# Which chunks are streamed: a third value chunk for an output pair, and another chunk in PSUM

## The chip, the cores and the metric

The kernel runs on one core of one Trainium2 chip. The metric is the device time of the whole program in microseconds (us); lower is better. The median of three runs of the kernel before is 2106.07 us (2104.05 to 2109.13).

## What is computed

Two independent halves are concatenated. Half A is a long convolution done by FFT in matmul form; it fills the first part of the time and the change does not touch it. Half B is a recurrent attention over 64 segments of 32 tokens; each segment is attended together with 8 memory rows that the segment before has produced:

```python
for s in range(n_seg):                       # 64 segments, one after the other
    h = concat([mem, x[:, 32*s:32*s+32]])    # 8 memory rows + 32 tokens, width 1024
    q, k, v = h @ Wq, h @ Wk, h @ Wv         # 32 heads of 128 each
    p = softmax(mask(q @ k.T * 128**-0.5))
    o = (p @ v) @ Wo                         # back to width 1024
    mem = o[:, :8]
    outs.append(o[:, 8:])
```

The four weight matrices have 1024 x 4096 bf16 elements each, 8 MB apiece, 32 MB in all; each segment needs all of them, and not all fit on the chip.

## The kernel before

**Weights.** The weights are cut into pairs: tiles of 128 x 2 x 1024 bf16, 512 KB. There are 64: `("qk", g, i)`, the i-th of eight chunks of the query and key weights of head group g (four groups of eight heads); `("v", G, i)`, the i-th of eight chunks of the value weights of half G (heads of groups 2G and 2G+1); and `("o", g, i)`, the i-th of four output pairs of group g. Below, qk26 is `("qk", 2, 6)`, v05 is `("v", 0, 5)`, o32 is `("o", 3, 2)`. They are kept in three ways:

- 45 pairs are resident in SBUF for the whole loop.
- 17 pairs are streamed from DRAM in every segment (`STREAM`, L40): 7 of qk, 5 of v, 5 of o. The qk and o ones are read from copies `Wstqk`, `Wsto` that stage 2 writes in one piece each (`relay`, L122); the value ones straight from the input `Wv`.
- 2 pairs are parked in PSUM (`PARKED`, L41): v02 and qk16. In every segment ScalarE (L762) and VectorE (L763) each copy one half of such a pair from PSUM into the ring (`unpark`).

**Ring.** Streamed and parked pairs pass through a ring `wring` of five slots. When the PE has used a pair of the ring, `done` (L768) gives its slot away at once: `PARKED` names the pairs at whose use the slot goes to a parked pair (the copy is noted and done at the next `unpark()`); otherwise `place` (L686) issues the transfer of the next streamed pair on SP's queue. Streamed pairs come in the order of their use.

**Order of a segment** (written out by hand, L948 to L1034). The PE runs: qk of group 0; the first half of v (chunks 0 to 3); transposes of q and k of group 0 (`tr_a`); qk of group 1 chunks 0 to 3; scores of group 0; qk of group 1 chunks 4 to 7; v chunks 4 to 7; `tr_a` of group 1; qk of group 2, with the scores of group 1 in the middle and the first product of probabilities and values (`pv`, L901) behind; qk of group 3 with the scores of group 2; the second half of v with `pv(u1)` and the scores of group 3; then the output products (`wo`, L916) of groups 0 to 3 with `pv(u2)` and `pv(u3)` between them. Behind each score matrix a chain of VectorE and ScalarE follows: maximum and subtraction (L866, L867), exponentials (ScalarE, L875), sum, reciprocal, product, transpose (L879 to L884), and four block copies into `PB` (L894). ScalarE also evacuates the accumulators (`qks` L801, `vsb` L816, `OT` L905) and the segment's result `Y_sb` (L1026), whose transpose `mt_tp` (L935) gives the next segment's `hT` its memory rows. The next segment's tokens (tile `H`) come by a transfer that is issued after the last scores, and are transposed into `x_tp` (L927).

`unpark()` stands at two places of the segment: inside qk of group 0, behind its fifth chunk (for v02), and behind `tr_a` of group 0 (for qk16).

**First segment.** The last few resident output pairs (`n_o`) are loaded within segment 0, ahead of other transfers on SP's queue, at `first_loads(1)`, `(2)` and `(3)` (L950): three pairs.

Of the kernel before, what the change touches and what calls it, by code (L numbers as in the profile page):

```python
# [21 lines left out]
def fused_kernel(ctx: ExitStack, tc, q, k, v, shift_k, ssm_k, ssm_D, outa, x, mem0, Wq, Wk, Wv, Wo, outb, n_seg):  # L22
# [14 lines left out]
    NS = 17  # L37
    scale = 128.0 ** -0.5
    RING = 5
    STREAM = {"qk": ((2, 4), (3,), (2, 6), (2, 6)), "v": ((0, 3, 5), (1, 5)), "o": ((2,), (1,), (0, 3), (2,))}  # L40
    PARKED = {("qk", 0, 4): ("v", 0, 2), ("v", 0, 3): ("qk", 1, 6)}  # L41

    msched = tc.manual_schedule()
    msched.__enter__()
# [10 lines left out]
    def keys(m, g, r):  # L55
        return [(m, g, i) for i in r]
# [3 lines left out]
    pairs += [key for g in range(4) for key in keys("o", g, range(4))]  # L60
    streamed = [key for key in pairs if key[2] in STREAM[key[0]][key[1]]]
    parked = list(PARKED.values())
    resident = [key for key in pairs if key not in streamed and key not in parked]
# [38 lines left out]
    to_open = sorted(resident, key=lambda key: (key not in early, first.get(key, 96)))  # L102
    wide = {}

    def open_res(n):
        if n:
            pool = cw_.enter_context(tc.tile_pool(name=f"b_wres{len(to_open)}", bufs=1))
            if not wide:
                wide["t"] = pool.tile([128, 8, 2, 1024], BF, name="Wearly")
            for _ in range(n):  # L110
                res_pool[to_open.pop(0)] = pool
# [89 lines left out]
    def rows_view(ap2d, t):  # L201
        return ap2d.rearrange("(p r) d -> r p d", r=16)[t]
# [437 lines left out]
    with ExitStack() as c3:  # L640
        io = c3.enter_context(tc.tile_pool(name="a3_io", bufs=3, side="right"))
        wk = c3.enter_context(tc.tile_pool(name="a3_wk", bufs=2, side="right"))
        ps_big = c3.enter_context(tc.tile_pool(name="a3_ps", bufs=3, space=PSUM))
        open_res(6)
        zts = {}

        def load_z(t):
            if t < 16:
                zt = io.tile([128, 2, 1024], BF, tag="zt", name="zt")
                nc.sync.dma_start(zt[:], SZ.rearrange("m (h r) d -> r m h d", h=2)[t])  # L650
                qt = wk.tile([128, 1024], BF, tag="qt", name="qt", bufs=3)
                nc.sync.dma_start(qt[:], rows_view(q, t))
                zts[t] = zt, qt

        halves = [(key, n) for key in parked for n in range(2)]
        park_w = []
        load_z(0)
        load_z(1)
        rows.load_to(rows.at // 16 * 8 + 16)
        rows.go(4)  # L660
        for t in range(16):
            load_z(t + 2)
            rows.half(4 if t < 6 else 1)
            zt, qt = zts[t]
            pt = ps_big.tile([128, 1024], F32, tag="big", name="y_ps")
            for hf in range(2):
                for h in range(2):
                    nc.tensor.matmul(pt[:, hf * 512:(hf + 1) * 512], lhsT=G2h[h][:, :],
                                     rhs=zt[:, h, hf * 512:(hf + 1) * 512], start=(h == 0), stop=(h == 1))
            ot = wk.tile([128, 1024], BF, tag="ot", name="ot")  # L670
            nc.vector.tensor_tensor(out=ot[:], in0=pt[:], in1=qt[:], op=ALU.mult)
            if t == 14:
                rows.load_to(96)
                for key, n in halves:
                    park_w.append(pring.tile([128, 1024], BF, tag="pring", name="park_w"))
                    nc.sync.dma_start(park_w[-1][:], half_src(key, n))
            nc.sync.dma_start(rows_view(outa, t), ot[:])
# [48 lines left out]
            nc.sync.dma_start(t[n], half_src(key, n))  # L726

    late_o = [key for key in resident if key[0] == "o"]
    assert len(late_o) == 11 and len(to_open) == 11
    rows.half(6, "AD")  # L730
    for i, (key, n) in enumerate(halves):
        tw = ps_p.tile([128, 1024], BF, tag="pp", name="park_t")
# [15 lines left out]
    for key in late_o[:8]:  # L748
        to_open.remove(key)
    n_o = late_o[8:]  # L750
    open_res(3)
    act = cw_.enter_context(tc.tile_pool(name="b_act", bufs=1))
    act2 = cw_.enter_context(tc.tile_pool(name="b_act2", bufs=2))

# [4 lines left out]
    def unpark():  # L759
        while to_copy:  # L760
            key, t = to_copy.pop(0)
            nc.scalar.copy(t[:, 0, :], park[key][0][:])  # L762
            nc.vector.tensor_copy(t[:, 1, :], park[key][1][:])  # L763
# [4 lines left out]
    def done(key):  # L768
        if key in res:
            return  # L770
        if key in PARKED:
            t = ring.tile([128, 2, 1024], BF, tag="wring", name="wring")
            placed[PARKED[key]] = [t[:]]
            to_copy.append((PARKED[key], t))
        else:
# [38 lines left out]
    def v_out():  # L814
        v = act.tile([128, 2, 256], BF, tag="vsb", name="vsb")
        nc.scalar.copy(v[:].rearrange("p n x -> p (n x)"), vacc[0][:])  # L816
        return v
# [7 lines left out]
    def tr_a(u):  # L825
        tp = transposes(u.qks)
        tv = tp[:].rearrange("e (j t c r) -> e t c j r", j=4, t=2, c=2)
        QK = acte.tile([128, 8, 72], BF, tag="qks", name="QK")
        u.QT, u.KT = QK[:, :, 0:32], QK[:, :, 32:72]
        nc.gpsimd.tensor_copy(u.KT[:, :, 32:40], u.qkb.rearrange("e (h t r) -> e t h r", h=8, t=2)[:, 1])  # L830
        nc.scalar.copy(u.QT.rearrange("e (c j) r -> e c j r", c=2), tv[:, 0])  # L831
        nc.scalar.copy(u.KT[:, :, 0:32].rearrange("e (c j) r -> e c j r", c=2), tv[:, 1])
# [6 lines left out]
    def new_u(g):  # L839
        u = G()  # L840
        u.g = g
        u.qkb = qkb[:, g, :]
        return u
# [96 lines left out]
    def new_hT():  # L940
        return acte.tile([128, 8, 32], BF, tag="hT", name="hT")
# [6 lines left out]
    for s in range(n_seg):  # L948
        last = s + 1 == n_seg
        def first_loads(g):  # L950
            for key in (n_o[g - 1:g] if s == 0 and g else ()):
                for n in range(2):
                    res_half(key, n)

        first_loads(0)
        us = [new_u(g) for g in range(4)]
        u0, u1, u2, u3 = us
        qk_part(u0, range(0, 5))
        unpark()
        qk_part(u0, range(5, 8))  # L960
        qk_out(u0)
        v_part(0, range(0, 4))
        tr_a(u0)
        unpark()
        first_loads(1)
        qk_part(u1, range(0, 4))
        S = scores(u0)
        softmax(u0, S)
        if s == 0:
            nc.vector.memset(PB[:], 0.0)  # L970
        blocks(u0, "DDDD")
        qk_part(u1, range(4, 8))
        qk_out(u1)
        v_part(0, range(4, 8))
        tr_a(u1)
        u0.v = u1.v = v_out()
        first_loads(2)
        qk_part(u2, range(0, 4))
        S = scores(u1)
        softmax(u1, S)  # L980
        if last:
            spare = [key for key in resident if key[0] != "o" and key[1] < 1 + (key[0] == "qk") and key not in early]
            for key, at in zip([key for key in streamed if key[0] == "o"], spare):
                nc.sync.dma_start(res[at][:], Wst[key])
                res[key] = res[at]
            for s0, s1 in ((0, 32), (32, s)):
                nc.sync.dma_start(OLs[:, s0:s1].rearrange("e s h r -> e (s h r)"),
                                  OLd[:, s0:s1].rearrange("e s x -> e (s x)"))
        qk_part(u2, range(4, 8))
        qk_out(u2)  # L990
        pv(u0, s)
        blocks(u1, "DDDD")
        first_loads(3)
        qk_part(u3, range(0, 2))
        tr_a(u2)
        qk_part(u3, range(2, 6))
        S = scores(u2)
        softmax(u2, S)
        qk_part(u3, range(6, 8))
        qk_out(u3)  # L1000
        v_part(1, range(0, 1))
        pv(u1, s)
        blocks(u2, "DDDD")
        v_part(1, range(1, 2))
        tr_a(u3)
        v_part(1, range(2, 5))
        S = scores(u3)
        if not last:
            H = load_h(s + 1)
            qkb = load_b(s + 1)  # L1010
        softmax(u3, S)
        v_part(1, range(5, 8))
        u2.v = u3.v = v_out()
        Y = ps_a.tile([128, 512], F32, tag="a", name="yacc")
        wo(u0, Y)
        pv(u2, s)
        blocks(u3, "DDAA")
        wo(u1, Y)
        wo(u2, Y)
        pv(u3, s)  # L1020
        if not last:
            hT = new_hT()
            h_rows(H, hT, 8)
        wo(u3, Y)
        Y_sb = act.tile([128, 256], BF, tag="P", name="Y_sb")
        nc.scalar.copy(Y_sb[:], Y[:, 0:256])  # L1026
        if not last:
            fill_mem(hT, Y_sb)
        for dq in range(4):
            nc.gpsimd.dma_start(outb[32 * s:32 * s + 24, dq * 256:(dq + 1) * 256], Y_sb[32 * dq + 8:32 * dq + 32, :])  # L1030
        if not last:
            load_vb(s + 1)
# [88 lines left out]
```

## Time and profile before

| | before |
|---|---|
| median of three runs | 2106.07 us (2104.05 to 2109.13) |
| the profiled execution | 2093.32 us, span 2091.5 us, granted clock 0.984 |
| PE, DVE, ACT, POOL busy | 81%, 53%, 43%, 20% of the span |
| read from HBM, written | 673.5 MB, 56.6 MB: 349 GB/s over the span |
| transfers into the ring | 448 of Wstqk, 320 of Wv, 315 of Wsto, 512 KB each |
| copies from PSUM into the ring | 128 on ScalarE (mean 1021 ns), 128 on VectorE (mean 692 ns) |
| end of Y_sb of the first and of the last segment | 416.7 and 2025.4 us after the span's start |

The profile is of one execution, which was somewhat faster than the median of the runs. The loop over the segments takes about 1609 us from the first Y_sb to the last, 25.5 us for one segment; the rest is half A with the first loads, and a last stage (L1044) of some 60 us.

### The profile page before, as it was taken

To read this page: it belongs to the slowest core of one execution; us is meant where nothing else is said; L and a number is where in the kernel's file an instruction comes from. 1 tells how busy PE (TensorE), PEld (TensorE's weight loads), DVE (VectorE), ACT (ScalarE), POOL (GpSimd) and SP (SyncE) were. 2 spreads that over 40 slices of the span, in tenths; PEclk is the share of its full clock that TensorE was granted. 3 is DMA by queue.
4 is the path that set the end of the run, shared out by engine and by line. 5 is a ranking of instruction groups with operands and counts; after the bars stand their busy time and mean duration, and the time that the engine had idled before them with its cause. 6 is when DMAs were issued, how large, how long until landed. Compare 5 with 4: busy or idle time off the path is not lost. (4 is left out here: it accounts for less than half of the span.)

```text
span 2091.5 us, 73911 instructions
## 1 busy us (share of the span) xinstructions
PE 1702.4 (81%) x30484; PEld 894.2 (43%) x30514; DVE 1115.3 (53%) x3313; ACT 908.7 (43%) x2276; POOL 413.1 (20%) x1018
## 2 busy tenths in 40 slices
PE   5888987888788888888887878888888878888879
PEld 2433233444444444444444444444444444444449
DVE  6986833355555555555555555555555555555541
ACT  5556731244444444444444444444444444444430
POOL 2004730121111111111111111111212121111110
PEclk9999999999999999999999999999999999999999
DMA  6899989999999999999999999999999999999980
GB/s 236 282 346 362 343 287 381 352 377 372 356 375 368 365 360 370 372 366 375 358 368 353 367 358 372 359 377 358 371 358 378 363 352 351 374 370 379 368 337 23
DMA packets 266384, 728.64 MB, mean 348 GB/s; under 512 B 65007, under 2 KB 77183, under 8 KB 265277
## 3 DMA queue, kind: packets, MB, share of 16 engines
q1 hardware_dynamic: 239486, 686.65, 88.8%
q0 software_dynamic: 15520, 22.06, 3.3%
q10 hardware_dynamic: 11040, 15.21, 2.1%
q8 instruction: 239, 3.92, 0.7%
q14 instruction: 99, 0.81, 0.1%
HBM read 673.52 MB, written 56.56 MB: 349 GB/s over the span
## 5 line engine op out<-in xcount | busy, mean ns | idle before, releaser
L795 PE MATMUL qkacc<-Wqk,hT 128*32 128x512 bf16 x4096 | 338.5, 383 | 0.0
L795 PEld LDWEIGHTS <-hT 128*32 128x32 bf16 x8192 | 184.9, 96 | 236.3 <-issue 84.2
L916 PEld LDWEIGHTS <-OT 128*32 128x32 bf16 x8192 | 210.1, 96 | 109.5 <-issue 59.2
L795 PE MATMUL qkacc<-wring,hT 128*32 128x512 bf16 x2048 | 204.9, 389 | 31.3 <-DMA wring<-Wstqk 25.5
L763 DVE COPY wring<-park 128x1024 bf16<-128x1024 bf16 x128 | 88.6, 692 | 239.4 <-PE vacc L809 124.8
L875 ACT ACTIVATE P<-S 128x128 bf16<-128x128 f32 x256 | 71.1, 278 | 330.4 <-DVE S L867 244.3
L809 PE MATMUL vacc<-Wv,hT 128*32 128x512 bf16 x2560 | 209.8, 382 | 0.0
L809 PE MATMUL vacc<-wring,hT 128*32 128x512 bf16 x1536 | 154.7, 387 | 65.5 <-DMA wring<-in_B_Wv_dram 63.6
L809 PEld LDWEIGHTS <-hT 128*32 128x32 bf16 x4096 | 113.0, 95 | 184.4 <-issue 108.3
L762 ACT COPY wring<-park 128x1024 bf16<-128x1024 bf16 x128 | 130.7, 1021 | 138.9 <-PE qkacc L795 112.8
L894 DVE COPY PB<-P 32x160 bf16<-32x160 bf16 x896 | 172.9, 193 | 10.6
L879 DVE TENSOR_REDUCE sm<-P 128x4 f32<-128x256 bf16 x256 | 107.5, 420 | 128.6 <-ACT P L876 128.6
L831 ACT COPY QK<-tp 128x256 bf16<-128x256 bf16 x256 | 95.4, 373 | 185.7 <-PE tp L822 184.5
L795 PE MATMUL qkacc<-Wearly,hT 128*32 128x512 bf16 x2048 | 161.0, 391 | 18.4 <-DVE hT L936 17.9
L830 POOL COPY QK<-qkb 128x64 bf16<-128x64 bf16 x256 | 61.3, 239 | 564.5 <-PE tp L822 404.8
L916 PE MATMUL yacc<-wring,OT 128*32 128x256 bf16 x2520 | 126.7, 274 | 37.4 <-DMA wring<-Wsto 35.2
L905 ACT CAST OT<-otacc 128x256 bf16<-128x256 f32 x256 | 98.7, 386 | 130.4 <-PE otacc L901 130.4
L801 ACT CAST qks<-qkacc 128x512 bf16<-128x512 f32 x256 | 151.1, 590 | 4.2 <-PE qkacc L795 3.5
L1030 POOL DMA_DIRECT2D out_dram<-Y_sb x256 | 129.1, 511 | 84.8 <-ACT Y_sb L1026 82.8
L822 PE MATMUL tp<-ident,qks 128*128 128x128 bf16 x1024 | 102.4, 223 | 52.6 <-ACT qks L801 50.3
L866 DVE TENSOR_REDUCE mx<-S 128x4 f32<-128x160 f32 x256 | 83.2, 325 | 85.2 <-PE S L863 79.5
L901 PE MATMUL otacc<-PB,vsb 128*128 128x160 bf16 x512 | 97.6, 238 | 35.3 <-ACT vsb L816 35.3
(212 smaller groups left out, 2957.1 us busy)
## 6 DMA issues: line engine op xcount, KB each, us to landing
wring<-Wstqk SPq DMA_DIRECT2D x448, 512.0 KB, 6.2
wring<-in_B_Wv_dram SPq DMA_DIRECT2D x320, 512.0 KB, 6.7
wring<-Wsto SPq DMA_DIRECT2D x315, 512.0 KB, 6.3
SK<-s_sb SPq DMA_DIRECT2D x8, 1024.0 KB, 5.5
SU<-s_sb SPq DMA_DIRECT2D x8, 1024.0 KB, 8.9
QKBd<-stq ACTq DMA_DIRECT2D x4, 2048.0 KB, 9.5
Kg<-SK SPq DMA_DIRECT2D x16, 512.0 KB, 7.0
Ug<-SU SPq DMA_DIRECT2D x16, 512.0 KB, 8.3
```

The source lines that it names most:

```text
L762: nc.scalar.copy(t[:, 0, :], park[key][0][:])
L795: nc.tensor.matmul(u.qk[p0:p0 + 32, :], lhsT=hT[:, kc, :], rhs=w[:, t, c2 * 512:(c2 + 1) * 512], start=(kc == 0), stop=(kc == 7), tile_pos ...
L801: nc.scalar.copy(u.qks[:], u.qk[:])
L809: nc.tensor.matmul(vacc[0][32 * c:32 * c + 32, :].rearrange("p (n x) -> p n x", n=2), lhsT=hT[:, kc, :], rhs=w[:, :, c * 256:(c + 1) * 256 ...
L822: nc.tensor.transpose(tp[:, j * 128:(j + 1) * 128], src[:, j * 128:(j + 1) * 128], ident[:])
L831: nc.scalar.copy(u.QT.rearrange("e (c j) r -> e c j r", c=2), tv[:, 0])
L879: nc.vector.tensor_reduce(out=sm[:], in_=Pv.rearrange("p b x k -> p x b k"), op=ALU.add, axis=AX.XY)
L894: (nc.vector if by[c] == "D" else nc.gpsimd).tensor_copy(to, src)
L901: nc.tensor.matmul(o, lhsT=w[:, i * 128:(i + 1) * 128], rhs=PB[:, 2 * kb + i].rearrange("p c q -> p (c q)"), start=(kb == 0), stop=(kb == 1))
L905: nc.scalar.copy(u.OT[:].rearrange("e (c i) q -> e i c q", i=2), ov[:, :, :, 0:32])
L916: nc.tensor.matmul(Y[32 * dq:32 * dq + 32, 0:256], lhsT=u.OT[:, hh, 0:32], rhs=w[:, hh % 2, dq * 256:(dq + 1) * 256], start=(u.g == 0 and ...
L1030: nc.gpsimd.dma_start(outb[32 * s:32 * s + 24, dq * 256:(dq + 1) * 256], Y_sb[32 * dq + 8:32 * dq + 32, :])
```

## The change

The set of streamed chunks, the second parked chunk and its place change; the number of streamed pairs (17), of parked pairs (2) and of slots (5) stays.

- Streamed qk: 2 and 4 of group 0, now 3 and 6 of group 1 (qk16 was parked), now 2 of group 2 (qk26 becomes the parked one), 2 and 6 of group 3.
- Streamed v: 0, 3, 5 of half 0 as before; 1, 3, 6 of half 1 in the place of 1, 5.
- Streamed o: the third pair of every group, four, in the place of o02, o11, o20, o23, o32.
- Parked: v02 as before, given the slot of qk04; qk26 in the place of qk16, given the slot of v05 in the place of that of v03. Its `unpark()` moves from behind `tr_a` of group 0 to behind `tr_a` of group 1, ahead of `v_out()`.
- One resident value pair fewer and one resident output pair more. So one pair fewer is opened at the start of stage 3, one more ahead of the loop, and `first_loads(3)` loads two pairs in the place of one.

```diff
-    STREAM = {"qk": ((2, 4), (3,), (2, 6), (2, 6)), "v": ((0, 3, 5), (1, 5)), "o": ((2,), (1,), (0, 3), (2,))}
-    PARKED = {("qk", 0, 4): ("v", 0, 2), ("v", 0, 3): ("qk", 1, 6)}
+    STREAM = {"qk": ((2, 4), (3, 6), (2,), (2, 6)), "v": ((0, 3, 5), (1, 3, 6)), "o": ((2,), (2,), (2,), (2,))}
+    PARKED = {("qk", 0, 4): ("v", 0, 2), ("v", 0, 5): ("qk", 2, 6)}
...
-        open_res(6)
+        open_res(5)
...
-    open_res(3)
+    open_res(4)
...
-            for key in (n_o[g - 1:g] if s == 0 and g else ()):
+            for key in (n_o[g - 1:g + g // 3] if s == 0 and g else ()):
...
         v_part(0, range(0, 4))
         tr_a(u0)
-        unpark()
         first_loads(1)
         qk_part(u1, range(0, 4))
...
         v_part(0, range(4, 8))
         tr_a(u1)
+        unpark()
         u0.v = u1.v = v_out()
```

More of the change, by code (lines that the diff above doesn't have):

```diff
@@ L728, in fused_kernel @@
     late_o = [key for key in resident if key[0] == "o"]
-    assert len(late_o) == 11 and len(to_open) == 11
+    assert len(late_o) == 12 and len(to_open) == 12
     rows.half(6, "AD")
```

## The prediction

> **What bounds the kernel now.** I read the page first (engine shares, GB/s per slice, the queues), then the stretch of the segment loop, the waits, the timeline of a segment, and last the issue and landing of every transfer into the ring. The page:
>
> ```profile
> PE 1702.4 (81%) x30484; PEld 894.2 (43%) x30514; DVE 1115.3 (53%) x3313; ACT 908.7 (43%) x2276; POOL 413.1 (20%) x1018
> ...
> GB/s 236 282 346 362 343 287 381 352 377 372 356 375 368 365 360 370 372 366 375 358 368 353 367 358 372 359 377 358 371 358 378 363 352 351 374 370 379 368 337 23
> ```
>
> No engine is full, and from slice 7 to 38 (the 64 segments) the bytes flow at an even 350 to 380 GB/s. The stretch table (span, PE, PEld, DVE, ACT, POOL, clock, DMA share, GB/s) over the loop, and over two pieces of one segment:
>
> ```profile
> 420.00:2020.00 1600.00, 1304.49 (x27324) 693.79 (x27316) 841.11 (x2887) 704.76 (x1947) 305.47 (x876) 0.99 0.99 367
> ```
> ```profile
> 1000.70:1003.70 3.00, 2.19 (x34) 0.97 (x35) 0.88 (x2) 1.06 (x2) 2.37 (x5) 1.00 1.02 412
> ...
> 1005.70:1006.70 1.00, 1.00 (x20) 0.49 (x19) 0.66 (x1) 0.66 (x3) 0.24 (x1) 1.00 0.99 350
> ```
>
> The DMA engines are nearly always occupied (0.99), yet move 412 GB/s in one piece and 350 in another. The waits, longest in total:
>
> ```profile
> PE vacc L809 <- DMA wring<-in_B_Wv_dram: 63.6, 121, 1.8
> PE yacc L916 <- DMA wring<-Wsto: 35.2, 72, 1.6
> PE qkacc L795 <- DMA wring<-Wstqk: 25.5, 45, 1.7
> ```
>
> PE loses 124 us to the ring, 2.0 us a segment. A second cord runs through VectorE; the timeline of its instructions in one segment:
>
> ```profile
> 1010.18 0.81 DVE L894 COPY PB<-P 32x160 bf16<-32x160 bf16 x4
> 1011.03 0.33 DVE L866 TENSOR_REDUCE mx<-S 128x4 f32<-128x160 f32 x1
> ```
>
> The softmax of one head group starts the moment the blocks of the one before are copied: from the first to the fourth, 3.7 us each, DVE and ACT go hand over hand with no air.
>
> Between the ends of Y_sb (L1026) a segment takes 25.53 us on average. Per streamed chunk, in us after the Y_sb end that opens the segment (medians over the segments of the trace; issue of its transfer, landing, first matmul, and PE's mean wait there; qk13 is query/key group 1, chunk 3; p is a copy from PSUM):
>
> ```
>        issue  land   use  wait          issue  land   use  wait
> qk02   -6.36  0.15  1.07  .01    qk32    6.38 12.06 12.61  .03
> qk04   -4.59  1.44  1.50  .10    qk36    7.42 13.61 13.88  .06
> v00    -3.80  2.88  2.92  .35    v11     8.10 14.92 15.22  .05
> v02p       -     -  3.35    -    v15     9.77 16.64 17.25  .00
> v03    -2.63  4.45  4.45  .62    o02    11.11 18.01 18.40  .04
> qk13   -0.64  5.90  5.93  .09    o11    13.07 19.26 20.15  .00
> qk16p      -     -  6.93  .04    o20    14.37 20.56 20.88  .05
> v05     1.50  7.37  7.60  .02    o23    15.68 22.13 22.05  .25
> qk22    3.37  9.07  9.32  .09    o32    18.05 24.13 24.20  .23
> qk26    3.88 10.52 10.65  .09
> ```
>
> Landings come every 25.5/17 = 1.50 us. Each transfer goes out about 0.44 us after the first matmul on the chunk whose slot it takes (o: 0.75), and lands 5.5 to 7.3 us after its issue. So the loop is a ring of five slots turning at the pace of the transfers, with the wait gathered where chunks lie densest (v00, v03, o23, o32).
>
> **The change, part by part.** Streamed pairs per segment: 7+5+5 = 17 before, 7+6+4 = 17 after; copies two and two. Bytes of the loop do not change; only the order does.
>
> *Early half.* After, the order is qk02, qk04, v00, v02p, v03, qk13, qk16, v05, qk22, qk26p, qk32, qk36, v11, v13, v16, o02, o12, o22, o32. The second copy has moved from seventh to tenth place, so one more transfer must land before v05. At the old cadence the landing at 7.37 is now qk16, wanted at 6.93 (0.44 late), and that at 9.07 is v05, wanted at 7.60: 1.47 late, the 0.44 contained in it. The issue tells the same: v05 now takes v00's slot, is issued at 3.37 and cannot land before about 3.37+5.5 = 8.9. Everything up to qk22 shifts by that; qk22's own 0.09 disappears.
>
> *Late half.* From the copied qk26 on, each chunk has a landing in hand. PE's waits from qk26 to o32, .09+.03+.06+.05+.04+.05+.25+.23 = 0.80, can go. But for o23's part the transpose of the next rows (L927) stands behind: H lands at 22.97 on average, x_tp starts at 23.20, so only 0.2 of it is to be had.
>
> *VectorE copy* (L763, 692 ns). Before, it lies in an idle gap ahead of the first softmax and costs nothing. After, it lies between the block copies of u0 and mx of u1, where the air is 0.14 us on average: 0.55 if S(u1) keeps its time. But S(u1) comes after v05; if v05 makes it 0.55 or more later, the copy is hidden behind that wait. So the larger of the two counts, not both.
>
> *ScalarE copy* (L762, 1.02 us). Before, ahead of the exponentials of u0, with 0.6 us idle behind it. After, ahead of v_out: vsb ends at 11.25 instead of 10.34, and pv(u0) wants it at 11.40. Hidden by 0.15; without that cover up to 0.9.
>
> *Sum for a segment.* PE's side: +1.47 − 0.09 − 0.80 = +0.58 if the waits at the segment's head (qk04, v00, v03, qk13: 1.16) stay, −0.58 if all go. They go in part: the head's transfers now follow o02, o12, o22, used 1.75, 0.3 and 0.5 us ahead of o11, o20, o23. DMA's side bounds the gain: with the engines at 0.99, at most 0.01×25.5 = 0.25 (more only if the slow pieces count as idle, see the rivals). So −0.25 to +0.58. Within it: five slots make 5×25.5 = 127.5 slot-us, of which the transfers hold 107 (17 × 6.3). The copy's slot was held from 4.9 to 7.4 (2.5) and is now held from v05's release at 8.04 to qk26's at 11.1 (3.05): +0.58, a fifth of it, 0.12, per segment; and late chunks now sit landed in their slots for up to 1 us longer, which can starve the queue again. I take +0.25, between 0.12 and 0.58: over 63 segments +15.8 us.
>
> The loop moves 9.29 MB a segment (17 pairs of 512 KB and 0.38 MB of small transfers): 367 GB/s over the loop, 412 in the piece above. By the latter rate alone the bytes would take 22.5 us of the 25.53, so time is lost to order, which is what the change alters. The Trainium skill, HBM Reference (Specifications (TRN2)), gives about 358 GB/s as one core's share of HBM; by that the bytes alone would take an estimated 26 us and the change would be worth nothing. The same page says that a core streaming alone goes well over its share; the trace's 412 GB/s agree with that sentence.
>
> *v for o.* The third value chunk is read straight from Wv. Medians issue to landing are 6.7 (in_B_Wv_dram) against 6.3 (Wsto), but the places in the queue differ. Between landings, v takes 1.51 us on average, o02, o11 and o20 1.38; a price of 0 to 0.13 a segment, 0 to +8 us; I take +1.
>
> *Before and after the loop.* One relay pair fewer in stage 2 (two POOL transfers with 0.5 MB read and written, behind other work): 0 to −3, I take −0.5. Segment 0 loads one resident output pair more, ahead of the ring on SP: one cadence, +1.5, or 0 if the ring has a lead. The last segment moves 13+4 pairs instead of 12+5: nothing.
>
> Sum +18. The profiled execution took 2093.3 us (span 2091.5), the median of the runs is 2106.1; a difference carries over: 2093 → 2111, 2106 → 2124. I round down to 2122, since the bounds below zero were rated at nothing.
>
> **Rivals.** *Saturated queue, no change:* if the slow stretches come from the memory and not from empty queues, 17 transfers take what they took, wherever PE waits: 2106 ± 4. For it: the share of 0.99. Against: 350 beside 412 GB/s. This is also where the share of HBM in the Trainium skill, HBM Reference, would lead; the 412 GB/s are over it.
>
> *Faster:* the dip at 5 to 7 us of a segment follows a gap in issues: between −0.64 and 3.37 only v05 goes out, because a copy and a late v03 hold slots. After, slots there go to transfers only (qk16, v05, qk22). Folded over 55 segments, the packets give 282 and 325 GB/s in the sixth and seventh us against 398 in the first: 0.29+0.18 = 0.47 us of transfer lacking. Filling it for good would give −30; a third, if the late half gives the rest back, −10: 2096. It decides if the late chunks are used within 0.3 us of landing, as now.
>
> *Chain-bound, much slower:* v05's wait is not given back and the softmax cord moves by 0.58 to 0.69 (the whole DVE copy) a segment: +37 to +43, 2143 to 2149. It decides if the head's waits stay at 1.1.
>
> **Numbers.** A measurement of this kernel tells some 0.2% (4 us) from nothing. Forecast 0.53 (2111 to 2134), no change 0.16, faster 0.15, chain-bound 0.16. So faster 0.15, same 0.16, slower 0.69. The range leaves out half of the outer cases: 2098 to 2142.
>
> **What would show it.** In the profile after: waits of L809 on in_B_Wv_dram up from 63.6 to 90 or more, most of the growth at v05; a wait of L795 on Wstqk at qk16; waits of L916 on Wsto below 15; the L763 copy straight after the block copies of u0, and an idle gap after it before mx of u1 (if there is none, the copy is the bound and not v05); GB/s of the loop 1% lower. I am wrong if v05 lands by 8.0, if L916 still waits 30 us, or if the loop's GB/s rise.

## The result: 5.7% slower

The median after is 2222.0 us (2207.8 to 2236.9, six runs) against 2104.4 us (2098.3 to 2109.1, six runs) of the kernel before: a ratio of 1.057 (95% interval 1.052 to 1.063). The profiled execution took 2220.2 us (span 2218.5, granted clock 0.958), 127 us more than that of before. The forecast was 2122 with 2142 as its upper end: the sign was right, and so was the place of the first delay, v05; the size was off by a factor of seven. Times of a segment below are read from one profiled execution of each kernel; it lies within 9 us of the kernel's median (0.14 us a segment), except for the kernel before (11 us below) and e3 (18 us above, 0.29 a segment).

### The profile after

The page: the shares of the engines, and the rate in the 40 slices.

```profile
PE 1738.0 (78%) x30484; PEld 894.9 (40%) x30514; DVE 1118.9 (50%) x3313; ACT 915.2 (41%) x2276; POOL 408.4 (18%) x1016
...
GB/s 241 291 334 348 309 358 316 371 353 338 357 325 333 356 347 327 325 357 338 349 329 364 331 349 341 360 349 343 337 337 344 332 338 332 346 352 334 346 280 21
```

PE, DVE and ACT run the same number of instructions; what has grown is PE's busy time, by 36 us. The rate in the loop's slices fell from between 350 and 380 to between 325 and 364 GB/s. The stretch table over the loop (columns as in the prediction: stretch, length, PE, PEld, DVE, ACT, POOL, clock, DMA share, GB/s):

```profile
420.00:2020.00 1600.00, 1247.84 (x25520) 646.70 (x25519) 787.20 (x2685) 663.97 (x1811) 284.78 (x822) 0.96 0.95 343
```

343 GB/s for 367, with the share of busy DMA engines down only from 0.99 to 0.95. The waits (us in total, times, longest):

```profile
DVE mx L866 <- PE S L863: 307.8, 125, 7.6
...
PE vacc L809 <- DMA wring<-in_B_Wv_dram: 141.4, 141, 14.2
...
PE x_tp L927 <- DMA H<-in_B_x_dram: 68.5, 61, 2.8
...
PE qkacc L795 <- DMA wring<-Wstqk: 34.9, 67, 1.3
...
PE yacc L916 <- DMA wring<-Wsto: 11.9, 25, 2.4
```

The wait for value chunks has more than doubled (63.6 before), that for o has nearly gone (35.2 before), and a new one stands in its place: PE waits 68.5 us for the tokens of the next segment, in nearly every segment. The same line before:

```profile
PE x_tp L927 <- DMA H<-in_B_x_dram: 10.6, 19, 1.8
```

DVE, which had no air ahead of the second softmax, now waits 308 us for scores (79.5 before): PE is late, not DVE. One segment (start, duration, instruction, idle time before it and what ended it), DVE's part first:

```profile
979.93 0.81 DVE L894 COPY PB<-P 32x160 bf16<-32x160 bf16 x4
981.06 0.69 DVE L763 COPY wring<-park 128x1024 bf16<-128x1024 bf16 x1 [0.32 <-PE vacc L809]
983.01 0.33 DVE L866 TENSOR_REDUCE mx<-S 128x4 f32<-128x160 f32 x1 [1.25 <-PE S L863]
```

and PE's in the same microseconds:

```profile
978.04 0.40 PE L795 MATMUL qkacc<-wring,hT 128*32 128x512 bf16 x4 [0.61 <-DMA wring<-Wstqk]
...
980.62 0.40 PE L809 MATMUL vacc<-wring,hT 128*32 128x512 bf16 x4 [1.74 <-DMA wring<-in_B_Wv_dram]
```

PE waits 0.61 at qk16 and 1.74 at v05. The copy into the ring runs behind v05's first matmul, and after it DVE still idles 1.25 us until the scores of u1: the copy is hidden behind v05, as forecast.

### Where the 127 us lie

From the ends of Y_sb (L1026) in both traces:

```
                                   before    after   difference
first Y_sb                         416.7     423.3     +6.6
62 segments, mean                   25.56     27.34  +110  (62 x 1.78)
last segment                        24.0      40.4    +16.4
after the last Y_sb                 66.2      59.9     -6.3
```

Per streamed chunk (medians over the segments, in us after the Y_sb end; PE's mean wait), as in the table of the prediction:

```
       issue  land   use  wait          issue  land   use  wait
qk02   -7.22 -0.18  1.07  .00    qk32    4.66 11.97 14.37  .00
qk04   -6.28  1.12  1.50  .05    qk36    6.00 13.25 15.42  .00
v00    -4.45  2.53  2.72  .14    v11     7.42 14.61 16.55  .00
v02p       -     -  3.15    -    v13    11.71 16.64 18.18  .00
v03    -3.33  3.83  4.18  .44    v16    13.01 18.30 19.20  .01
qk13   -0.64  5.31  5.57  .01    o02    14.77 19.85 20.10  .09
qk16    1.50  6.91  6.98  .46    o12    15.80 21.38 22.10  .00
v05     3.19  9.32  9.32 1.46    o22    16.95 22.98 23.20  .07
qk22    3.71 10.59 11.23  .04    o32    18.58 24.70 26.07  .00
qk26p      -     - 12.54  .07
```

Ahead of v05 only qk16 is later than it was, by 0.05. v05 is used 1.72 us later than before (9.32 for 7.60), and o32, the last one, still 1.87 later (26.07 for 24.20): nothing of the delay comes back. And the chunks behind v05 now lie landed in their slots: from landing to use, the 17 transfers of a segment held 7.3 us of slot time before and hold 15.7 now (means; the table has medians). Five slots make 5 x 27.34 = 136.7 slot-us a segment: 17 x 6.34 of transfer, 15.7 of lying landed, the rest, 13.2, of use and of the parked pairs; before it was 127.8 = 17 x 6.36 + 7.3 + 12.4. The 8.4 slot-us more, a fifth of them for each slot, are 1.7 us of the 1.78 a segment. The transfers in flight, 17 x 6.34/27.34, are 3.94 on average, for 4.22.

That is a balance and not yet a cause: its terms add up to the segment by their definition. It says where the slots are while PE is late, not why PE does not catch up.

The same for PE, from one Y_sb end to the next (mean of 62 segments, us):

```
                                   before    after   difference
PE busy                             20.82    21.32    +0.50
waits for ring transfers             2.08     2.77    +0.69
wait for H (x_tp)                    0.17     1.10    +0.93
other waits                          2.48     2.14    -0.34
```

So the waits for the ring are less than half of the growth; the largest single part is the wait for the next segment's tokens.

### The profile page after: what moved, and what is told of

Read it like the earlier page. It is cut to its first block, busy times and chain, and to the rows that moved or that the text cites. A ratio compares the mean times of both kernels' runs of the same rounds, so it can differ in the third digit from the quotient of the medians.

```text
span 2218.5 us, 73975 instructions
## 1 busy us (share of the span) xinstructions
PE 1738.0 (78%) x30484; PEld 894.9 (40%) x30514; DVE 1118.9 (50%) x3313; ACT 915.2 (41%) x2276; POOL 408.4 (18%) x1016
## 4 chain that ended last, share of the span: by engine, by line
DMA 43%; PE 37%; DVE 7%; ACT 7%; issue 3%; SPq 0%; POOL 0%; ACTq 0%; DVEq 0%; POOLq 0%
DMA wring<-in_B_Wv_dram 27%; PE qkacc L795 12%; DMA H<-in_B_x_dram 9%; PE vacc L809 6%; PE yacc L916 3%; PE tp L822 3%; PE otacc L901 3%; PE pl L1044 3%; ACT wring L762 2%; PE ps_q L181 1%; PE ps_k L181 1%; DMA wring<-Wstqk 1%; DMA wring<-Wsto 1%; DMA zt<-SZ 1%; DMA pring<-in_B_Wq_dram 1%
## 5 line engine op out<-in xcount | busy, mean ns | idle before, releaser
L795 PE MATMUL qkacc<-Wqk,hT 128*32 128x512 bf16 x4096 | 353.9, 400 | 0.0
L809 PE MATMUL vacc<-wring,hT 128*32 128x512 bf16 x1792 | 180.1, 392 | 142.7 <-DMA wring<-in_B_Wv_dram 141.4
L795 PEld LDWEIGHTS <-hT 128*32 128x32 bf16 x8192 | 185.5, 98 | 261.5 <-issue 118.4
L795 PE MATMUL qkacc<-wring,hT 128*32 128x512 bf16 x2048 | 213.3, 406 | 40.2 <-DMA wring<-Wstqk 34.9
L916 PEld LDWEIGHTS <-OT 128*32 128x32 bf16 x8192 | 210.4, 97 | 58.4 <-issue 26.0
L809 PE MATMUL vacc<-Wv,hT 128*32 128x512 bf16 x2304 | 226.1, 396 | 0.0
L809 PEld LDWEIGHTS <-hT 128*32 128x32 bf16 x4096 | 107.9, 96 | 275.6 <-issue 204.7
L795 PE MATMUL qkacc<-Wearly,hT 128*32 128x512 bf16 x2048 | 167.1, 405 | 18.4 <-DVE hT L936 17.9
L1030 POOL DMA_DIRECT2D out_dram<-Y_sb x256 | 128.9, 510 | 127.8 <-ACT Y_sb L1026 120.6
L884 DVE STREAM_TRANSPOSE P<-P 128x256 bf16<-128x256 bf16 x256 | 114.0, 445 | 8.8
```

The source lines that it names most:

```text
L795: nc.tensor.matmul(u.qk[p0:p0 + 32, :], lhsT=hT[:, kc, :], rhs=w[:, t, c2 * 512:(c2 + 1) * 512], start=(kc == 0), stop=(kc == 7), tile_pos ...
L809: nc.tensor.matmul(vacc[0][32 * c:32 * c + 32, :].rearrange("p (n x) -> p n x", n=2), lhsT=hT[:, kc, :], rhs=w[:, :, c * 256:(c + 1) * 256 ...
L884: nc.vector.transpose(out=Pf, in_=Pf)
L916: nc.tensor.matmul(Y[32 * dq:32 * dq + 32, 0:256], lhsT=u.OT[:, hh, 0:32], rhs=w[:, hh % 2, dq * 256:(dq + 1) * 256], start=(u.g == 0 and ...
```

## The experiments

The theory formed from this: the ring has no slot to spare. A pair landed early keeps a slot from the next transfer, so that a delay at v05 is handed round the ring and not worked off; what the price is depends on how much lead each stretch of the order has. Its rivals: the third value chunk and the exchange of o for v are the price (the bytes' source, not the order); the copy of the parked chunk in its new place is (VectorE); the memory is saturated. Kernels named "from e3" and so on carry that kernel's edit too.

### Which half of the change: e1 and e2

e1 is the kernel after with the streams of v and o as before (and the counts of opened pairs with them), so the parked chunk and its place alone are moved; e2 the kernel after with qk16 parked in its old place (the streams of v and o alone).

```diff
 # e1, against after
-"v": ((0, 3, 5), (1, 3, 6)), "o": ((2,), (2,), (2,), (2,))
+"v": ((0, 3, 5), (1, 5)), "o": ((2,), (1,), (0, 3), (2,))
 # e2, against after
-"qk": ((2, 4), (3, 6), (2,), (2, 6))
+"qk": ((2, 4), (3,), (2, 6), (2, 6))
-("v", 0, 5): ("qk", 2, 6)
+("v", 0, 3): ("qk", 1, 6)
...
         tr_a(u0)
+        unpark()
...
         tr_a(u1)
-        unpark()
```

> Only the second parked chunk changes (qk26 at the use of v05, its copy behind tr_a of group 1, qk16 streamed); value and output streams as before. Head theory (one more transfer must land before v05, 1.7 us a segment, and the late half gives nothing back): +100 to +115 us, some 2205 to 2220; v05 waits over 1 us a segment; the first and last segments as before. Rival, the third value chunk read from Wv is what costs: within 10 us of 2104.

> Only the streamed sets of v and o change (1, 3, 6 of half 1; four output pairs); the parked chunk and its copy as before. Head theory: the loop keeps 25.5 us a segment; the last segment is longer by some 14 us (the transfer of v16 stands behind the loads for the last stage) and the first by some 3: 2115 to 2128. Rival, value chunks are dear: the loop grows by 1 us or more a segment, over 2165.

Measured: e1 2195.8 us, ratio 1.043 (1.037 to 1.049); e2 2111.5, 1.004 (1.001 to 1.007). The segment takes 27.20 us in e1 and 25.67 in e2, for 25.56 before. In the stretch tables, before, e1, e2:

```profile
430.00:2010.00 1580.00, 1287.85 (x26968) 685.68 (x26971) 828.09 (x2843) 694.97 (x1916) 303.25 (x866) 0.99 0.99 366
```
```profile
430.00:2010.00 1580.00, 1232.54 (x25296) 641.02 (x25292) 776.73 (x2668) 656.81 (x1798) 280.05 (x812) 0.97 0.96 343
```
```profile
430.00:2010.00 1580.00, 1299.66 (x26872) 681.53 (x26868) 834.70 (x2845) 696.34 (x1915) 299.48 (x861) 0.98 0.99 365
```

and e2's wait for value chunks:

```profile
PE vacc L809 <- DMA wring<-in_B_Wv_dram: 63.9, 109, 15.8
```

So the parked chunk alone makes 1.64 of the 1.78 us, and the rate falls with it; by the medians e1 has 92 of the 118 us, somewhat below its forecast. The streams alone cost 0.11 a segment in the trace, too little to be told from nothing. But e2 has the long last segment (41.6 us; e1 25.5): the longest wait of that line, 15.8 us, stands there.

### The last segment: e3

After, the timeline of SP's queue in the last segment, and PE's wait:

```profile
2129.17 0.33 SPq L691 DMA_DIRECT2D wring<-in_B_Wv_dram  x1
2129.56 0.87 SPq L984 DMA_DIRECT2D Wv<-Wsto  x1
2130.48 1.37 SPq L984 DMA_DIRECT2D Wqk<-Wsto  x3
2132.03 1.15 SPq L987 DMA_DIRECT2D Wearly<-OLd  x2
2133.57 0.33 SPq L691 DMA_DIRECT2D wring<-in_B_Wv_dram  x1
```
```profile
2151.10 0.62 PE L809 MATMUL vacc<-wring,hT 128*32 128x512 bf16 x4 [14.18 <-DMA wring<-in_B_Wv_dram]
```

The first line is v13's transfer, the last v16's. In the kernel before, the last ring transfer (v15, the second of the first line) goes out ahead of the transfers of L984:

```profile
2009.10 1.90 SPq L691 DMA_DIRECT2D wring<-in_B_Wv_dram  x2
2011.06 0.43 SPq L984 DMA_DIRECT2D Wv<-Wsto  x1
```

v16 is now the last ring transfer of the program, and is issued later in the segment (13.0 us after Y_sb) than v15 was (9.8). It falls behind the block of the last segment that loads four output pairs and two large pieces of OLd (L984, L987), and its 512 KB land behind them. e3 moves that block behind `qk_out(u2)`:

```diff
         softmax(u1, S)
-        if last:
-            ...
         qk_part(u2, range(4, 8))
         qk_out(u2)
+        if last:
+            ...
```

> The kernel after, with the loads for the last stage issued behind qk of group 2 in the last segment, so that the transfer of v16 goes out ahead of them. If the 14 us wait in the last segment is a queue matter: 8 to 14 us faster than the kernel after (some 2208 to 2214), with some of it lost to the wait for the last rows ahead of L1044. Rival, the wait was hiding those loads: within 3 us of the kernel after.

Measured: 2203.9 us, ratio 1.050 (1.043 to 1.057); the last segment takes 25.3 us for 40.4, and the stretch behind it 65.6 for 59.9, since OLd now is waited for again. So 15.1 back and 5.7 lost, by the traces. The intervals of the ratios overlap with those of after (1.052 to 1.063); the place is shown by the trace, the gain in time only as its middle. The loop is as it was: its 27.50 come from the slowest of four executions (2222 us, granted clock 0.948; the others 2192 to 2207 at 0.961 to 0.964), and an estimate from the median, 18 us less over 63 segments, is 27.2. Gains against e3's trace are therefore too large by some 0.3, and the medians are given beside them. The kernels below build on e3.

### One landing fewer ahead of v05: e5, e13, e14

e5 keeps qk16 resident and streams qk24 instead, so that v05's transfer is not behind qk16's.

```diff
 # against e3
-"qk": ((2, 4), (3, 6), (2,), (2, 6))
+"qk": ((2, 4), (3,), (2, 4), (2, 6))
```

> As e3_last_fixed, but qk16 is resident and chunk 4 of group 2 is streamed in its place: the same 17 streams, the same copies at the same places (qk26 in v05's slot, VectorE copy ahead of the softmax of u1), and one transfer fewer that must land before v05. Head theory: v05's wait falls under 0.2 us a segment and the time to 2100 to 2130. Rival, the place of the copies or the slot held by qk26 costs: it stays within 20 us of e3_last_fixed.

Measured: 2168.4 us, 1.032 (1.028 to 1.036); 26.58 us a segment. The waits:

```profile
PE vacc L809 <- DMA wring<-in_B_Wv_dram: 93.0, 170, 1.9
...
PE yacc L916 <- DMA wring<-Wsto: 45.6, 103, 1.9
```

v05's mean wait is down from 1.38 in e3 to 0.20, and still only 0.92 of the 1.94 us come back (by the medians 35.5 us, 0.56 a segment); neither of the two forecasts was met. The late half starves instead. No transfer is issued between 6.00 us and 9.46: v05's slot is with the parked chunk, and the other four carry transfers under way, of which the first, qk22, lands at 8.67. v11, v13 and v16 then land 2.0 and 1.6 us apart, and PE waits at o02 (0.38). Lying landed is not the price here: the 17 pairs do so for 7.5 us a segment, as in the kernel before (7.3), but a transfer takes 6.59 us from issue to landing for 6.35.

e14 takes the other way to an early v05: v02's copy gets v00's slot in the place of qk04's, so that the transfers ahead go out earlier.

```diff
 # against e3
-PARKED = {("qk", 0, 4): ("v", 0, 2), ...
+PARKED = {("v", 0, 0): ("v", 0, 2), ...
...
-        qk_part(u0, range(0, 5))
-        unpark()
-        qk_part(u0, range(5, 8))
+        qk_part(u0, range(0, 8))
         ...
-        v_part(0, range(0, 4))
+        v_part(0, range(0, 1))
+        unpark()
+        v_part(0, range(1, 4))
```

> e3_last_fixed, but v02 is copied into the slot of v00 in place of qk04's, so that the transfer of v05 goes out at the use of qk04, 1.2 us sooner; v02's copy now has two chunks' time only and PE may wait up to 1 us for it. Head theory: v05 lands 0.8 to 1.2 us sooner after its neighbours and its wait falls from 1.5 to under 0.8; the time falls by 10 to 50 us, 2155 to 2195, unless the wait for the copy eats it. Rival, v05 is late because the queue is full and not because it is issued late: its landing stays at 9.3 and the time within 10 us of 2204, or above it.

Measured: 2167.1 us, 1.032 (1.026 to 1.038), 26.57 a segment. v05 lands at 8.24 and PE waits 0.47 for it, but 1.03 for the copied v02, whose copy now comes late. The wait is moved, not removed. Of the value chunks' transfers little wait is left:

```profile
PE vacc L809 <- DMA wring<-in_B_Wv_dram: 35.3, 61, 1.6
```

That line alone would have promised a faster kernel than before (63.6 there); the segment is 1.0 us longer.

e13 is e5 with the parked chunk given a later slot, that of qk22, and copied after the first four chunks of group 2 of qk:

```diff
 # against e5
-("v", 0, 5): ("qk", 2, 6)
+("qk", 2, 2): ("qk", 2, 6)
...
         tr_a(u1)
-        unpark()
...
         qk_part(u2, range(0, 4))
+        unpark()
         S = scores(u1)
```

> e5_thin_head, but qk26 is given the slot of qk22 in place of v05's, and copied ahead of the scores of u1. So v05's slot goes to the transfer of v11 at once (issue near 7.7 in place of 9.5 us) and qk26 holds a slot for some 2 us in place of 3.3; the copies now lie in front of the softmax of u1 on both engines. Slot theory: the gap in issues goes and with it the empty queue from 11 to 17 us; 0.5 to 0.9 us less a segment, 2110 to 2140. Rival, the dip comes from somewhere else: 2155 or more.

Measured: 2155.6 us, 1.027 (1.024 to 1.030); 26.49 a segment, 0.09 less than e5. The gap in the issues stays (v11 at 7.76, the next at 10.71): it is only held by another chunk. By the medians it is 12.7 us, 0.2 a segment, where 0.5 to 0.9 were expected of a later slot: that it is v05's slot which is held is at most a small part of the rest of the price. What a slot held for a copy at all costs here, e13 doesn't tell, since it still holds one.

### The copy on VectorE: e9

e9 is e5 with the VectorE copy of qk26 cut to 64 of 1024 columns, GpSimd filling the others with zeros; the attention of group 2 is thereby left incomplete.

```diff
 # against e5
+            n = 64 if key[0] == "qk" else 1024
...
-            nc.vector.tensor_copy(t[:, 1, :], park[key][1][:])
+            nc.vector.tensor_copy(t[:, 1, 0:n], park[key][1][:, 0:n])
+            if n < 1024:
+                nc.gpsimd.memset(t[:, 1, n:1024], 0.0)
```

> e5_thin_head with VectorE copying 64 of the 1024 columns of its half of qk26 from PSUM (the rest is set to zero by GpSimd, so the attention of group 2 is not the reference's). VectorE theory: the 0.69 us copy ahead of the maximum of u1 moves the softmax chain by 0.5 us and H with it; without it 0.4 to 0.7 us less a segment, 2125 to 2143. Rival, the slot: qk26 holds v05's slot for 3.3 us so that v11 goes out at 9.5 in place of 7.8, and the queue runs empty behind it; then it stays at 2160 to 2170 (e5: 2168).

The tile view of the parked pairs (duration min/median/max in ns, first and last start, forms):

```profile
L764 DVE COPY wring<-park x128: 190/441/693, 390.5 to 2100.1; 128x1024 bf16<-128x1024 bf16 x64, 128x64 bf16<-128x64 bf16 x64
```

Half of the copies last 0.19 us instead of 0.69, and the time does not fall: 2172.7 us, 1.034 (1.030 to 1.038), 26.86 a segment for e5's 26.58. PE does not wait for the zeros either (0.00 us at qk26). VectorE's copy is not the price.

### The tokens of the next segment: e7 and e8

x_tp waits 1.1 us a segment for H in after (0.17 before). H is issued 1.6 us later within the segment, as everything behind v05 is, and takes 5.9 us from issue to landing for 4.9 (medians), though it goes out on ScalarE's queue and not behind the ring's transfers. The move sets x_tp behind the last output products, in e3 (e7) and in the kernel before (e8):

```diff
-        hT = new_hT()
-        h_rows(H, hT, 8)
         wo(u3, Y)
+        hT = new_hT()
+        h_rows(H, hT, 8)
```

> e3_last_fixed with the transposes of the next rows (x_tp, the consumer of H) moved behind the last output products, so that H has 1 us longer to land. If the wait for H (1.1 us a segment) is what keeps the late half from giving time back: 0.6 to 1.0 us less a segment, 2140 to 2167. Rival, the time is set by the ring all round and another wait takes its place: within 12 us of e3_last_fixed (2204).

> The kernel before with only x_tp moved behind the last output products. H lands 0.2 us ahead of x_tp on average there, with 19 waits: -0.1 to -0.3 us a segment where the ring lets it, 2086 to 2098; if the ring sets the pace, 2100 to 2106.

Measured: e7 2154.9 us, 1.026 (1.022 to 1.030), 26.56 a segment for e3's 27.50; e8 2101.5, 1.002 (0.999 to 1.004), 25.64. What x_tp waited for, from the tile view of e3 and of e7 (us, times):

```profile
  DMA H<-in_B_x_dram: 72.1, 60
```
```profile
  DMA H<-in_B_x_dram: 0.2, 1
```

The wait goes, and with it 0.94 us a segment by the traces, 49 us or 0.8 a segment by the medians: most of the 1.1 of the wait. In the kernel before there was hardly such a wait to take, and e8 is no faster.

### How many slots: e15

The kernel before with one slot fewer puts a price on a slot.

```diff
-    RING = 5
+    RING = 4
```

> The kernel before with four slots in the ring in place of five. It prices a slot. If slots held idle are what starves the queue, a fifth fewer slots costs several us a segment: 28 to 31 us a segment, 2260 to 2450. If the queue is full anyway, under 1 us a segment: below 2165.

Measured: 2354.1 us, 1.121 (1.116 to 1.127), 29.64 a segment. The stretch table and the waits:

```profile
430.00:2010.00 1580.00, 1191.87 (x23272) 613.66 (x23272) 718.46 (x2464) 603.30 (x1658) 258.51 (x746) 0.93 0.92 316
```
```profile
PE yacc L916 <- DMA wring<-Wsto: 152.1, 145, 3.3
...
PE vacc L809 <- DMA wring<-in_B_Wv_dram: 143.4, 134, 15.6
```

A slot is worth 4.1 us a segment. The transfers in flight fall to 3.27, 23% fewer, and each takes 5.71 us, 10% less than the 6.36 of five slots: the rate follows the number in flight for the greater part, so at these rates the memory is not what sets it alone. The 8.4 slot-us that after loses are 0.33 of a slot of 25.56 us, by this price an estimated 1.3 us of the 1.78. The granted clock falls too (0.93), by an edit that touches the ring alone, so a lower clock can follow from PE's waits and need not be a cause of its own. It may add to them: PE's busy time is 21.3 us a segment after (1247.84 x 27.34/1600) for 20.8 before.

### Where the value chunks are read from: e16, e17, e18, e19

Value pairs are read from Wv in rows of 4 KB that lie 8 KB apart; the others from copies in one piece. Here stage 2 copies the value pairs too, in the kernel before (e16), in e3 (e17), in e5 (e18), and in e11 (e19), which is introduced below. (Lines of these kernels lie three higher: L806 is vacc.)

```diff
-    relaid = [key for key in streamed if key[0] != "v"]
+    relaid = list(streamed)
...
-    for m, g, i in streamed:
-        if m == "v":
-            Wst[m, g, i] = Wv[...]
...
-                relay(1)
+                relay(2)
```

> The kernel before, with the streamed value pairs copied in stage 2 to tiles in one piece (as those of qk and o are) and read from there; stage 2 has five pairs more to copy, 0 to 15 us. If rows of 4 KB at a step of 8 KB out of Wv are slow to read: 0.3 to 1.0 us less a segment, a segment of 24.6 to 25.2 us. If the source does not matter: 25.4 to 25.7 us a segment and a time at or above 2104.

> e3_last_fixed with the value pairs copied likewise (six). Source theory: v05, v13 and v16 no longer land 1.6 to 2.4 us behind their forerunners but some 1.35; the segment falls from 27.4 to 26.0 to 26.8 us, the time to some 2125 to 2175. Slot theory: within 0.2 us a segment of e3_last_fixed, 2195 to 2220.

> e5_thin_head with the value pairs copied likewise. There the issues of v11, v13 and v16 lie close together and they land 1.6 to 2.0 us apart. Source theory: the segment falls from 26.6 to 25.3 to 25.9 us, the time to 2095 to 2135. Slot theory: 26.4 or more a segment, 2155 or more.

```
                      us    ratio (95%)               segment  without the copies
e16 (before)       2099.3   1.000 (0.996 to 1.003)     25.43        25.56
e17 (e3)           2168.9   1.033 (1.030 to 1.036)     26.53        27.50
e18 (e5)           2131.6   1.016 (1.012 to 1.020)     25.84        26.58
```

e17 and its wait for value chunks:

```profile
430.00:2010.00 1580.00, 1256.78 (x25922) 654.32 (x25918) 797.21 (x2723) 672.02 (x1838) 290.71 (x834) 0.97 0.97 352
```
```profile
PE vacc L806 <- DMA wring<-Wstv: 82.9, 117, 3.2
```

In the order of after the source costs 0.97 us a segment (e3) and 0.74 (e5), in that of before 0.13. By the medians, with the later start set aside, it is some 0.7, 0.8 and 0.2. In e18 v11, v13 and v16 land 1.6 and 1.45 us apart (2.0 and 1.6 in e5). Why the same source costs more in one order than in the other isn't shown. That three value transfers follow one another in the late half, where before there were two, is not it: e11 (below) has the three as well, with the parked chunk in its old place, and there the copies gain 0.20 by the traces (25.21 to 25.01). The larger price goes with the parked chunk's new place. Before the loop the larger copy costs: the first Y_sb comes at 434.5 us in e17 for 424.1 in e3.

### Together: e20 and e21

e20 is e17 with x_tp late (the diff of e7), e21 is e18 with x_tp late.

> e17_after_v_copied with x_tp behind the last output products. If the price of the source and the wait for H are two separate terms, e7's 0.9 us a segment comes off again: 25.6 to 25.9 us a segment, 2110 to 2135. If they are one and the same (a slow queue makes H late): under 0.4 us, 2145 or more.

> e18_thin_head_v_copied with x_tp behind the last output products: all three remedies on the kernel after. If nothing else is wrong with the new place of the copy, 25.0 to 25.3 us a segment and 2078 to 2095, as e19_best_v_copied, which keeps the old place. If the place of the copy has a price of its own: 25.5 or more, over 2105.

Measured: e20 2140.1 us, 1.022 (1.017 to 1.027), 25.94 a segment, between its two forecasts; e21 2115.0, 1.009 (1.007 to 1.012), 25.63. So step by step from e3: 27.50, the source 26.53, the tokens 25.94, one landing fewer in the head 25.63. Each of these alone, taken from e3's trace, gives 0.92 to 0.97 us, and together they give 1.87; by the medians 0.6 to 0.8 each, and some 1.5 together. That they add up to less than their sum is seen without e3's trace in the tokens alone: the same move gives 0.59 behind e17, and 0.21 behind e18, where the head is thinner too. That the ring carries part of each wait to the next place would explain it, but isn't shown.

### Back to the old place, and a faster kernel: e11 and e19

e11 is e2 with the block of the last segment and x_tp moved (the diffs of e3 and e7): the new streams of v and o, qk16 parked where it was. e19 is e11 with the value pairs copied.

> e2_streams_only (2111) with the loads for the last stage behind qk of group 2, and x_tp behind the last output products. The first takes 12 to 16 us from the last segment, the second up to 0.5 us from each of the others (x_tp at 23.87, H landing at 23.83): 2070 to 2097. If both only move waits: 2105 to 2111.

> e11_streams_best with the value pairs copied likewise. Source theory: 0.3 to 1.0 us less than its 25.2 us a segment, 2035 to 2075 with the longer stage 2. Slot theory: at or above 2084.

Measured: e11 2083.8 us, 0.995 (0.992 to 0.997), 25.21 a segment; e19 2077.6 us, 0.990 (0.987 to 0.993), 25.01. e19:

```profile
430.00:2010.00 1580.00, 1312.18 (x27560) 701.30 (x27550) 850.93 (x2901) 707.78 (x1956) 308.57 (x882) 0.99 1.00 374
```

Both are faster than the kernel after, and than the kernel before by 0.5% and 1.0%, little but outside the intervals; e19's time lies between its two forecasts. e19 and e21 differ in the second parked chunk and what goes with it (qk16 in v03's slot, with qk26 streamed and qk24 resident, against qk26 in v05's slot, with qk24 streamed and qk16 resident): 25.01 against 25.63, so 0.62 us a segment belong to that exchange, with all other remedies in. On e5, e9 and e13 found no gain in a shorter VectorE copy and a small one at most in another slot than v05's; of what the 0.62 consist stays open.

## Why the prediction was wrong in size

**Right.** The early half, read off the table of landings: v05 was to land not before 8.9, at 9.07 by the cadence, and lands at 9.32; PE was to wait 0.44 at qk16 and waits 0.46; v05 was to be used 1.47 late, the 0.44 contained in it, and is used 1.72 late. (The wait at v05 alone, 1.46, is not the forecast's 1.47: it comes on top of the 0.46.) Both copies are hidden: vsb ends at 12.93 on average and pv(u0) starts at 13.33, and behind the VectorE copy there is the idle gap that was named as the sign that v05 is the bound. The waits of L916 are 11.9 us (below 15), those of L809 141 (90 or more). "Slower" had 0.69. One sign was far off: the loop's GB/s were to be 1% lower and are 6.5% lower (343 for 367).

**Wrong: "PE's waits from qk26 to o32 … 0.80, can go" and the head's 1.16 "go in part".** The waits did go from the ring: from qk32 to o32 0.17 are left, and of the head's 1.16 there are 0.64. But no time came with it. v05's 1.72 are 1.87 at o32. The prediction named one thing standing behind the last 0.2 of this, H, and left H where it was; H is issued behind the last scores, so it moves with v05, and it took 1 us longer on the way. Its wait grew by 0.93 us a segment, a term that the sum did not have; taking it away gave back 0.8 to 0.94 (e7). PE's busy time grew by 0.50, at a lower granted clock, and was not in the sum either. The ring's own waits grew by 0.69, near the 0.58 that stood at the upper end. That H would wait was to be seen before: a transfer that is issued at the end of the chain that is delayed can't be a fixed point to be worked towards.

**Wrong: "I take +0.25, between 0.12 and 0.58".** This was the decisive term, the price of a segment, and it measured 1.78. The balance of slots was set up (127.5 slot-us, 107 in transfers) and then only the copy's slot was entered, 0.58; the late chunks "up to 1 us" in their slots were mentioned as an afterthought. Moving the uses of the ten transfers behind v05 by the 1.47 already worked out, with their landings kept, gives 14.7 slot-us or 2.9 us a segment as an upper end; 8.4 came, nearly six tenths of it, and 1.78 was the price. The bound of 0.58 was PE's side of the sum with the head's waits left as they were; but it held only the ring's waits, with H landing when it did before.

**Wrong: the rival "chain-bound" as the far end.** It gave 43 us, one delay of 0.69 carried once through each segment. It had the right mechanism (v05's delay not given back) with the wrong size: the delay is the whole 1.47 and more (1.72 at v05, 1.87 at o32).

**Nearly right: "v for o … I take +1", of 0 to +8.** The streams of v and o cost 0.11 us a segment alone (e2, 25.67 for 25.56) and 0.14 on top of the parked chunk (27.34 for e1's 27.20), some 7 to 9 us by the traces and too little to be told from nothing. What the prediction did not price is another quantity, the source of all the value chunks: 0.1 to 0.2 us a segment in the old order (e16), 0.7 to 0.97 in the new one (e17).

**Wrong: "The last segment … nothing".** +16.4. By count that holds, 17 pairs either way; but SP's queue was not read there. The block ahead of which v15 was issued, and behind which v16 is, stands in the code, and the transfer that was last to be issued moved from 9.8 to 13.0 us.

**Wrong: the start, +1.5 − 0.5.** The first Y_sb comes 6.6 us later: 1.6 ahead of the loop, and 5.0 in segment 0. There `qkb`, which the scores wait for, is issued 6.7 us later (391.4 for 384.7), because the load of a parked half far ahead of it on SP's queue goes out late (363.1 for 356.8) and all behind it with it. One cadence of 1.5 us was allowed, for the additional output pair, which stands behind `qkb` in that queue. The delay comes with the streams of v and o: e2 has it as well (361.3; first Y_sb at 423.7), e1 has not (358.5; 418.4).

**The saturated queue.** The 412 GB/s were the argument against it, and the runs bear it out. e19's segment takes 25.01 us, at 374 GB/s over 1580 us. The Trainium skill, HBM Reference (Specifications (TRN2)), puts a core's share at about 358 GB/s; by that a segment of 9.29 MB would take an estimated 26 us at least. The measurement decides. It agrees with the page's other sentence, that a core streaming alone goes well above its share, though over the whole loop it is 4% above.

## What to carry to other kernels

For a ring of buffers, add up the slot time: transfers in flight, pairs landed and not yet used, pairs in use. Transfers in flight divided by the time of one is the rate, and while a pair lies landed its slot carries no transfer; a change of order is judged by that whole sum, not by the one chunk that comes late, and with the transfers' own time in it, which e5 shows can grow while the landed time does not. When a step is delayed, follow each transfer that is issued behind it, the small ones on other queues too, and read the queue order of the first and last turn of the loop separately.

## What was not expected of the hardware

- The time of a transfer depended little on how many were in flight: 6.36 us with 4.22 of them, 6.34 with 3.94, 5.71 with 3.27 (four slots). It also went with the order: 6.59 with 4.21 in e5. The rate goes with their number, 366, 343 and 316 GB/s, while the share of busy DMA engines falls only from 0.99 to 0.95 and 0.92.
- A transfer of 64 KB on another queue (H, ScalarE's) took 5.9 us after and 4.9 before, with the ring's transfers in another order.
- Reading value pairs in 4 KB rows 8 KB apart, rather than from one piece, cost 0.97 us a segment in one order and 0.13 in another (by the medians some 0.7 and 0.2).
- The granted clock went with the waits: 0.99 over the loop before, 0.96 after, 0.93 with four slots, 0.99 in e19.
